# Layer 2 of six chunks as seven half-block products, q's sums from a ones column, and a new written order

## The chip, the core and the metric

The kernel runs on one core of a Trainium2 chip. TensorE (PE) multiplies matrices from SBUF into PSUM; VectorE (DVE), ScalarE (ACT) and GpSimd (POOL) do elementwise work; SyncE (SP) and also ACT and POOL issue DMAs. PEld is TensorE's loading of the stationary operand, which has rows of its own in the profile. The metric is device time of one execution in microseconds (us), median of three runs. Before the change it is 292.93 us (292.82 to 293.19).

## The reference

For each of 8 batches and 8 heads (576 rows, 64 columns), an attention without a softmax over scores:

```python
q_s = softmax(q, axis=-1)            # over the 64 columns of a row
k_s = softmax(k, axis=2)             # over the 576 rows
kv  = einsum('bhsd,bhse->bhde', k_s, v)
a   = einsum('bhsd,bhde->bhse', q_s, kv)
```

The heads side by side make x (8 x 576 x 512). Then comes a feed-forward block:

```python
xn  = (x - mean(x)) / sqrt(var(x) + 1e-6) * g_ln
out = x + relu(xn @ w_ch1) @ w_ch2   # 512 -> 2048 -> 512
```

Inputs and output are float32; the kernel multiplies in bfloat16 and accumulates in float32.

## The kernel before, in words

A batch m is handled as a "side" (attention and normalization, class Side) and a chunk (the feed-forward). A side takes 512 of the 576 rows as four tiles j = 0..3 of 128; the 64 rows left over of batches m-1 and m form a fifth tile (j = 4) of the odd m. The eight chunks 0 to 7 have 512 rows each, and chunk 8 holds the left-over rows of all batches.

A side's steps, by their names in the written order: `kl`, `ql`, `vl` (loads; `kll`, `qll`, `vll` for left-over rows); `kmax`, `kmaxl`, `kar` (maximum of k, across partitions on POOL); `ksub`, `kexp`; `vc` (v to bfloat16, on POOL from batch 2 on); `qmax`, `qsub`, `qexp`; `qTd` (q transposed by a DMA on SP's queue, from batch 2 on); `pkv` (the products k'v, with a ones column in v for k's sums); `kvb` (scaled into `kv_ab`); `zq` (the row sums of exp(q) and their reciprocals: a DVE reduction, L353, and L354; for batches 0 and 1 two-column products `zpe` on PE and a reciprocal, L366); `po` (q times kv, L419 and L428, into one PSUM bank); `x` (L442, which divides by q's sums and writes x in bfloat16 and its row sum); `xn` (x minus its mean; DVE or ACT); `sq` (L466, ACT, sum of squares); `xT`/`xTd` (the transpose, by DMA from batch 2 on, L502); `rstd` (L506, L507).

A chunk's steps: `l1.c.m` (L538: four matmuls of 128 x 512 into one PSUM bank, for each of 16 groups m of 128 hidden columns; chunks 0 and 1 in smaller parts, L552); `relu` (L544, ACT, into `hT`); `l2.c.t` (L592: for each of four row tiles 16 matmuls of 512 columns, in four steps); `put` (L602, DVE: PSUM times rstd, minus x, which is held negated); `store` (one 256 KB DMA per tile). The normalization's rstd is thus applied at the end, in `put`, and no step before layer 2's end waits for it. Chunk 8 ends with three pieces of its last tile (L570, L578).

Nothing is scheduled by a tool while the kernel is built. The string PROGRAM lists every step, and the engines receive their instructions in that order, each engine's queue in order. `warm` steps are matmuls whose result nobody reads. `gate` steps are tiny DMAs on SP's queue that read a few elements of a tile, so that SP's queue waits until the tile is there. PSUM's eight banks are two rings of four (`mm_ps` for the feed-forward, `sm_ps` for the sides); v's float32 tile (`vin`) has two buffers, the output tile (`otp`) four.

Of the kernel before, what the change touches and what calls it, by code (L numbers as in the profile page):

```python
# [20 lines left out]
def kernel(  # L21
# [13 lines left out]
    P = 128  # L35
# [9 lines left out]
    INV = 1.0 / DM  # L45
    HALVED = ()
# [7 lines left out]
    ZPE = 2  # L54
# [39 lines left out]
    kv_ab = const.tile([P, 4, KO1, P], BF16)  # L94
# [33 lines left out]
    class Side:  # L128
# [199 lines left out]
        def qT_heads(self, c0, c1):  # L328
            ptr = self.ptr[c0] = sm_ps.tile([P, J, c1 - c0, P], BF16, tag="sm", name="ptr")
# [26 lines left out]
        def zpe(self, a, n):  # L356
            zp = self.zps[a] = sm_ps.tile([P, n, H], FP32, tag="sm", name="zp")
# [10 lines left out]
        def qT(self, a, n):  # L368
            ptr = self.ptr[a] = sm_ps.tile([P, n, KO1, P], BF16, tag="sm", name="ptr")
# [14 lines left out]
        def pkv(self, c0, c1):  # L384
            if c0 in (a for a, b in self.kvparts):
                self.pk = sm_ps.tile([P, KO1, KVW], FP32, tag="sm", name="pk")
# [14 lines left out]
        def kvb(self, a, b):  # L401
# [3 lines left out]
            for e in range(2):  # L405
                r = slice(64 * e, 64 * e + 64)
                nc.vector.tensor_mul(
                    kv_ab[r, self.m % 4, a:b, 64 * e:64 * e + 64], pk[r, a:b, :D],
# [3 lines left out]
        def po(self, j, ps=None):  # L412
            ps = ps or sm_ps
            pot = self.pot[j] = ps.tile(
                [P, H, D], FP32, tag="sm" if ps is sm_ps else "mm", name="pot"
            )
            if j < J:
                for c in range(KO1):
# [3 lines left out]
                        kv_ab[:, self.m % 4, c, :], start=True, stop=True,  # L422
                    )
            else:
                for b in (self.m - 1, self.m):
                    r = rows(b)
                    for c in range(KO1):
                        nc.tensor.matmul(  # L428
                            pot[r, 2 * c:2 * c + 2, :],
                            qTl[:, c, r],  # L430
                            kv_ab[:, b % 4, c, :], start=True, stop=True,
                        )

        def x(self, j):

            m = self.m
            if j < J:
# [3 lines left out]
            xs = xs_ab[:, m, j:j + 1]  # L441
            nc.vector.scalar_tensor_tensor(  # L442
                xt.rearrange("p (h d) -> p h d", h=H), in0=self.pot[j], scalar=-1.0,
                in1=rq[:, :, None].to_broadcast([P, H, D]),
# [4 lines left out]
        def xn(self, eng, j):  # L449

            xt, xs = self.xs[j]
            if eng is nc.scalar:
                eng.activation(  # L453
                    xn_ab[:, j], xt, AF.Identity, bias=xs, scale=-float(DM)
                )
            else:
                eng.tensor_scalar(
                    xn_ab[:, j], in0=xt, scalar1=-float(DM), scalar2=xs,
                    op0=ALU.mult, op1=ALU.add,
# [10 lines left out]
        def xT(self, a, n, c0=0, c1=KO1):  # L470
            pxt = self.pxt[a, c0] = sm_ps.tile([P, n, c1 - c0, P], BF16, tag="sm", name="pxt")
# [32 lines left out]
    def rstd_of(ci):  # L504
        ln = sm2.tile([P, J], FP32, tag="ln")
        nc.scalar.activation(ln, ssq[:, ci], AF.Ln, bias=eps_ln, scale=INV)  # L506
        nc.scalar.activation(rstd[:, ci], ln, AF.Exp, scale=-0.5)  # L507
# [26 lines left out]
    def l1(ci, m):  # L534
        src = xnT_ab[:, ci % 2] if ci < B else xnTl
        ph = phs[ci, m] = mm_ps.tile([P, SM], FP32, tag="mm", name="ph")
# [9 lines left out]
    def l1_part(ci, c, t, n):  # L546

        ph = phs[ci, c, t] = mm_ps.tile([P, 4 // n, n * P], FP32, tag="mm", name="ph")
# [14 lines left out]
    pcs = {}  # L563

    def l2_last(i):

        c, n = LAST[i]
        pcs[i, "last"] = mm_ps.tile([P, n], FP32, tag="mm", name="pc")
# [6 lines left out]
    def put_last(i):  # L575
        c, n = LAST[i]
        o = ots[i, "last"] = otp.tile([P, DM], FP32, tag="ot", name="ot")
        nc.vector.scalar_tensor_tensor(  # L578
            o[:, :n], in0=pcs[i, "last"], scalar=rstd[:, B, 3:], in1=xl[:, 3, c:c + n],
            op0=ALU.mult, op1=ALU.subtract,  # L580
        )

    def store_last(i):
        c, n = LAST[i]
        for eng, b in ((nc.sync, B - 2), (nc.scalar, B - 1)):
            eng.dma_start(out[b, SM:, c:c + n], ots[i, "last"][rows(b), :n])

    def l2(ci, ti, kos):
        if kos[0] == 0:
            pcs[ci, ti] = mm_ps.tile([P, DM], FP32, tag="mm", name="pc")  # L590
# [6 lines left out]
    ots = {}  # L597

    def put(ci, ti):
        xt = x_ab[:, ci % 2, ti] if ci < B else xl[:, ti]  # L600
        ots[ci, ti] = otp.tile([P, DM], FP32, tag="ot", name="ot")
        nc.vector.scalar_tensor_tensor(  # L602
            ots[ci, ti], in0=pcs[ci, ti], scalar=rstd[:, ci, ti:ti + 1], in1=xt,
# [3 lines left out]
    def store(eng, ci, ti):  # L607
        if ci in HALVED:
            dst = out[ci, (ti // 2) * 2 * P:(ti // 2 + 1) * 2 * P, :]
            eng.dma_start(dst.rearrange("(p j) c -> p j c", j=2)[:, ti % 2, :], ots[ci, ti])  # L610
        elif ci < B:
            dst = out[ci, :SM, :].rearrange("(p j) c -> p j c", j=J)
            eng.dma_start(dst[:, ti, :], ots[ci, ti])
        else:
            for b in (2 * ti, 2 * ti + 1):
                eng.dma_start(out[b, SM:, :], ots[ci, ti][rows(b)])

    def warm(n, width):

        for i in range(n):  # L620
            nc.tensor.matmul(
                idle[:, :width], ident, kv_ab[:, 3, :width // P], start=True, stop=True
# [23 lines left out]
        relu.0.1.0 l1.0.0.2 sq.0.1 qT.1.0 relu.0.1.2 l1.0.8.0 relu.0.0.2 l1.0.9.0 kmax.1.0
        l1.0.11.0 relu.0.9.0 relu.0.8.0 l1.0.10.0 relu.0.11.0 qTe.1.0@DV l1.0.13.0 relu.0.10.0
# [534 lines left out]
```

## Time and profile before

| | |
|---|---|
| median of three runs | 292.93 us (292.82 to 293.19) |
| span of the profiled execution, which is its own time from first to last instruction | 291.7 us |
| PE | 282.4 us busy |
| DVE | 182.0 us busy |
| ACT | 171.7 us busy |
| POOL | 45.9 us busy |
| granted TensorE clock | 0.999 |
| first matmul of chunk 0's layer 1 | at 21.2 us |
| last matmul of chunk 8 ends | at 287.6 us |

A group's row gives its line, engine and operation, what it writes and reads, the shape and the count, then the busy time and the mean duration of one, and after the bar how long the engine was idle before them and who ended that idle time. A matmul's duration includes the pipeline behind it, so the time from one matmul to the next is read from the chain of work: a piece of 16 matmuls that takes 3.45 us has one every 216 ns. DVE's groups add up to some 193 us where its busy time is 182.0: two instructions in a row overlap by about 36 ns. Times outside the span (some 1.2 us between span and median) are the same program's start and end.

### The profile page before, as it was taken

What the parts mean: (1) busy time and instruction counts of PE and PEld (TensorE: products, weight loads), DVE (VectorE), ACT (ScalarE), POOL (GpSimd) and SP (SyncE); (2) the same over time, 40 slices, a digit from 0 to 9 for tenths busy, and PEclk for the clock granted to TensorE, in tenths of its full rate; (3) what the DMA queues carried; (4) which work ended last, traced back from release to release, by engine and by line L of the source; (5) the groups of instructions that cost most, each with busy time, mean ns of one, the idle gap of its engine ahead of it and who ended that gap; (6) DMA issues with size and microseconds to landing.
All of it is one profiled execution on the core that took longest, in us unless ns stands there. A gap on an engine that the chain in (4) does not pass through costs nothing.

```text
span 291.7 us, 4966 instructions
## 1 busy us (share of the span) xinstructions
PE 282.4 (97%) x1923; PEld 145.8 (50%) x1952; DVE 182.0 (62%) x309; ACT 171.7 (59%) x322; POOL 45.9 (16%) x48
## 2 busy tenths in 40 slices
PE   6999999999999999999999999999999999999994
PEld 2479445756444544554454444544544444444443
DVE  6988696997999978988859759614520410220022
ACT  1578793587868885795485638860787077017400
POOL 1810420080421030115130300300000000000000
PEclk9999999999999999999999999999999999999999
DMA  7999999997989999697899759366202331110015
GB/s 213 332 247 237 237 223 298 353 227 205 218 225 216 310 190 246 151 277 170 231 175 281 215 128 235 53 91 143 76 18 51 77 125 39 67 40 36 2 30 115
DMA packets 78144, 49.62 MB, mean 170 GB/s; under 512 B 44580, under 2 KB 73640, under 8 KB 78120
## 3 DMA queue, kind: packets, MB, share of 16 engines
q1 hardware_dynamic: 61008, 34.75, 49.0%
q10 hardware_dynamic: 12888, 10.36, 12.3%
q0 software_dynamic: 4224, 4.19, 8.5%
q8 instruction: 15, 0.25, 0.4%
q14 instruction: 9, 0.07, 0.1%
HBM read 36.70 MB, written 9.44 MB: 158 GB/s over the span
## 4 chain that ended last, share of the span: by engine, by line
PE 74%; DMA 16%; DVE 2%; SPq 2%; ACT 2%; POOL 1%; issue 1%; POOLq 0%
PE pc L592 37%; PE ph L538 27%; DMA w_sb<-in_moe_w_ch_dram 8%; PE ph L552 5%; DMA qt<-in_q_dram 4%; DMA vt<-in_v_dram 3%; PE pot L419 2%; PE pk L394 1%; DMA vl<-in_v_dram 1%; PE pc L570 1%; POOL v_ab L109 1%; SPq L382 1%; DVE qm L295 1%; ACT hT L544 1%; DVE x_ab L442 1%
## 5 line engine op out<-in xcount | busy, mean ns | idle before, releaser
L592 PE MATMUL pc<-w_sb,hT 128*128 128x512 bf16 x544 | 122.8, 379 | 1.3 <-DMA w_sb<-in_moe_w_ch_dram 0.2
L544 ACT ACTIVATE hT<-ph 128x512 bf16<-128x512 f32 x112 | 63.3, 595 | 60.8 <-PE ph L538 59.9
L538 PE MATMUL ph<-xnT_ab,w_sb 128*128 128x512 bf16 x374 | 86.0, 379 | 0.4
L592 PEld LDWEIGHTS <-hT 128*128 128x128 bf16 x560 | 54.1, 98 | 64.3 <-DMA w_sb<-in_moe_w_ch_dram 0.7
L538 PEld LDWEIGHTS <-w_sb 128*128 128x128 bf16 x448 | 42.9, 98 | 49.0 <-issue 0.2
L602 DVE SCALAR_TENSOR_TENSOR ot<-pc,rstd,x_ab 128x512 f32<-128x512 f32 x32 | 23.2, 746 | 44.4 <-PE pc L592 32.9
L199 POOL PARTITION_ALL_REDUCE km<-kmx x10 | 17.0, 1697 | 88.7 <-DVE kmx L194 63.0
L552 PE MATMUL ph<-xnT_ab,w_sb 128*128 128x128 bf16 (+2 forms) x254 | 29.1, 272 | 0.1
L442 DVE SCALAR_TENSOR_TENSOR x_ab<-pot,rq 128x512 bf16<-128x512 f32 x32 | 20.9, 686 | 12.6 <-PE pot L419 12.4
L466 ACT ACTIVATE xsq<-x_ab,xs_ab 128x512 bf16<-128x512 bf16 x32 | 22.9, 715 | 6.3 <-issue 4.7
L552 PEld LDWEIGHTS <-w_sb 128*128 128x128 bf16 x256 | 19.7, 98 | 8.3 <-DMA w_sb<-in_moe_w_ch_dram 0.2
L109 POOL CAST v_ab<-vt 128x1024 bf16<-128x1024 f32 x14 | 18.7, 1356 | 23.3 <-DMA vt<-in_v_dram 23.2
L241 ACT ACTIVATE ek_ab<-kt 128x1024 bf16<-128x1024 f32 x14 | 14.5, 1051 | 10.8 <-DVE kt L217 10.7
L217 DVE TENSOR_TENSOR kt<-kt,km 128x1024 f32<-128x1024 f32 x14 | 17.7, 1275 | 3.7 <-POOL km L199 3.7
L559 ACT ACTIVATE hT<-ph 128x512 bf16<-128x512 f32 x32 | 17.5, 597 | 3.7 <-PE ph L552 3.7
L295 DVE TENSOR_REDUCE qm<-qt 128x16 f32<-128x1024 f32 x14 | 16.8, 1208 | 3.0 <-DMA qt<-in_q_dram 3.0
L453 ACT ACTIVATE xn_ab<-x_ab,xs_ab 128x512 bf16<-128x512 bf16 x23 | 15.7, 713 | 4.9 <-DVE x_ab L442 4.9
L300 DVE TENSOR_TENSOR qt<-qt,qm 128x1024 f32<-128x1024 f32 x14 | 17.8, 1274 | 0.2
L602 DVE SCALAR_TENSOR_TENSOR ot<-pc,rstd,xl 128x512 f32<-128x512 f32 x3 | 2.2, 748 | 22.0 <-PE pc L592 22.0
L305 ACT ACTIVATE eq_sb<-qt 128x1024 bf16<-128x1024 f32 x14 | 14.7, 1050 | 1.2 <-DMA xnT_ab<-xn_ab 1.0
L353 DVE TENSOR_REDUCE sumq<-eq_sb 128x16 f32<-128x1024 bf16 x12 | 14.4, 1201 | 0.0
L538 PE MATMUL ph<-xnTl,w_sb 128*128 128x512 bf16 x63 | 13.9, 379 | 0.1
(87 smaller groups left out, 203.7 us busy)
## 6 DMA issues: line engine op xcount, KB each, us to landing
qt<-in_q_dram SPq DMA_DIRECT2D x6, 1024.0 KB, 9.3
kt<-in_k_dram SPq DMA_DIRECT2D x5, 1024.0 KB, 7.2
vt<-in_v_dram SPq DMA_DIRECT2D x5, 1024.0 KB, 9.2
out_dram<-ot SPq DMA_DIRECT2D x20, 256.0 KB, 3.4
w_sb<-in_moe_w_ch_dram POOLq DMA_DIRECT2D x8, 512.0 KB, 15.9
out_dram<-ot ACTq DMA_DIRECT2D x12, 256.0 KB, 3.3
kt<-in_k_dram ACTq DMA_DIRECT2D x2, 1024.0 KB, 11.9
vt<-in_v_dram ACTq DMA_DIRECT2D x2, 1024.0 KB, 9.9
```

The lines of the kernel that those rows point to most:

```text
L109: eng.copy(dst, src) if eng is nc.scalar else eng.tensor_copy(dst, src)
L217: eng.tensor_tensor(a, a, b, op=ALU.subtract)
L295: nc.vector.tensor_reduce(t, self._q(a, n), axis=AX.X, op=ALU.max)
L300: eng.tensor_tensor(x, x, t[:, :, :, None].to_broadcast([P, n, H, D]), op=ALU.subtract)
L442: nc.vector.scalar_tensor_tensor(xt.rearrange("p (h d) -> p h d", h=H), in0=self.pot[j], scalar=-1.0, in1=rq[:, :, None].to_broadcast([P, ...
L466: nc.scalar.activation(xsq, xt, AF.Square, bias=xs, scale=-float(DM), accum_out=s)
L538: nc.tensor.matmul(ph, w1_sb[:, ko, m * P:(m + 1) * P], src[:, ko, :], start=(ko == 0), stop=(ko == KO1 - 1),)
L544: nc.scalar.activation(hT[:, m, :], phs[ci, m], AF.Relu)
L552: nc.tensor.matmul(ph[:, i], w1_sb[:, ko, m * P:(m + 1) * P], xnT_ab[:, ci % 2, ko, t * P:(t + n) * P], start=(ko == 0), stop=(ko == KO1 - 1),
L559: nc.scalar.activation(hT[:, c * (4 // n):(c + 1) * (4 // n), t * P:(t + n) * P], phs[ci, c, t], AF.Relu)
L592: nc.tensor.matmul(pcs[ci, ti], hT[:, ko, ti * P:(ti + 1) * P], w2_sb[:, ko, :], start=(ko == 0), stop=(ko == KO2 - 1),)
L602: nc.vector.scalar_tensor_tensor(ots[ci, ti], in0=pcs[ci, ti], scalar=rstd[:, ci, ti:ti + 1], in1=xt, op0=ALU.mult, op1=ALU.subtract,)
```

## The change

In chunks 2 to 7 (`QUICK`) layer 2 is computed by half blocks. Rows (512), the inner dimension (2048) and columns (512) are each halved. Eight products of 256 x 1024 by 1024 x 256 would give the four output blocks; the change forms seven products (`term` 1 to 7; Strassen's scheme in Winograd's form). Each is 16 matmuls of 256 columns, eight inner blocks for two row tiles. For that,

- four sums or differences of halves of `hT` (`sum.c.n.g`, in two parts g of 128 x 1024 bfloat16 on DVE, eight instructions a chunk) and, once, four of the halves of `w_ch2` (`ws`, 128 x 2048 bfloat16; three on POOL, one on DVE);
- the seven products go to three PSUM banks: products 1, 6, 7 and 4 add up in u, 2 in a, 5 and 3 in b. Between them DVE reads u minus x four times (`less`) and adds a or b three times (`plus`), all 128 x 512; each next product into u waits for the `less` that reads the one before;
- `put` falls away in these chunks, and rstd is multiplied in by `xn` instead. So `xn` waits for `rstd` of the four tiles and for two small instructions (`sc`, on POOL or DVE) in chunks 2 to 7;
- two stores of 512 KB a chunk replace four of 256 KB, and a `less` waits until the last chunk's store has read the output tile, of which there is now one per row tile.

For batches 1 to 7, q's sums come from a ones column in `kv_ab` (65 columns a head instead of 64): `po` writes 130 columns a matmul, over two PSUM banks, and `x` begins with a reciprocal of eight numbers from PSUM. The `zq` reduction and batch 1's `zpe` go.

The rings of PSUM are replaced by bank numbers in the order itself (`%n`). `vin` has one buffer. The whole PROGRAM is written anew: the layer-1 groups come in another order (in chunk 3: 0, 15, 12, 2, 6, ...), loads move between SP's and ACT's queues, and the gates stand early in SP's queue.

```diff
-            if j < J:
-                xt, rq = x_ab[:, self.sl, j], self.rq[:, j]
...
+            if m == 0:
+                rq = self.rq[:, j, :, None]
             else:
-                xt, rq = xl[:, m // 2], self.rql[:, 0]
+                rq = sm2.tile([P, H, 1], FP32, tag="rq2")
+                nc.vector.reciprocal(rq, self.pot[j][:, :, D:D + 1])
...
+            if ci in QUICK:
+                by, xs = (scale_ab[:, n, ci, i:i + 1] for n in range(2))
...
+    def scale_of(eng, ci, i=0, n=J):
+        r = rstd[:, ci, i:i + n]
+        xs = xs_ab[:, ci, :J] if ci < B else xs_ab[:, 2 * i + 1, J:]
+        eng.tensor_scalar(
+            scale_ab[:, 0, ci, i:i + n], in0=r, scalar1=-float(DM), scalar2=None, op0=ALU.mult
+        )
+        eng.tensor_tensor(scale_ab[:, 1, ci, i:i + n], r, xs, op=ALU.mult)
...
+    SUMS = {3: (S3, A[0][0], A[1][0], ALU.subtract), 2: (S2, A[1][1], S3, ALU.subtract),
+            1: (S1, S2, A[0][0], ALU.add), 4: (S4, A[0][1], S2, ALU.subtract)}
+    WSUMS = {1: (T1, W[0][1], W[0][0]), 2: (T2, W[1][1], T1), 3: (T3, W[1][1], W[0][1]),
+             4: (T4, W[1][0], T2)}
+    TERMS = {1: ("u", A[0][0], W[0][0]), 2: ("a", A[0][1], W[1][0]), 3: ("b", S4, W[1][1]),
+             4: ("u", A[1][1], T4), 5: ("b", S1, T1), 6: ("u", S2, T2), 7: ("u", S3, T3)}
...
+    def sums(eng, n, a, b):
+        o, x, y, op = SUMS[n]
+        eng.tensor_tensor(o[:, a:b], x[:, a:b], y[:, a:b], op=op)
...
+        for ko in range(KH):
+            for i in range(2):
+                nc.tensor.matmul(
+                    quick[ci, where][:, i], s[:, ko, i * P:(i + 1) * P], w[:, ko],
+                    start=first and (ko, i) == (0, 0), stop=(ko, i) == (KH - 1, 1),
...
+    def less_x(ci, where, t, c):
+        i = slice(2 * t, 2 * t + 2)
+        x = (x_ab[:, ci % 2, i] if ci < B else xl[:, i])[:, :, c * NH:(c + 1) * NH]
+        nc.vector.tensor_tensor(part(t, c), quick[ci, where], x, op=ALU.subtract)
+
+    def plus(ci, where, t, c):
+        o = part(t, c)
+        nc.vector.tensor_tensor(o, quick[ci, where], o, op=ALU.add)
...
+        l1.6.9%1 relu.6.1 l1.6.10%2 sum.6.3.0 relu.6.9 sum.6.3.1 relu.6.15 term.6.1%0 relu.6.10
+        sum.6.2.1 qexp.7.4 sum.6.2.0 sq.7.0 qTd.7.4 po.7.3%4 less.6.1 sq.7.1 x.7.3 xT.5.4 term.6.6
+        sq.7.2 sum.6.1.0 sq.7.3 sum.6.1.1 term.6.2%7 rstd.7 less.6.2 sc.7@DV xn.7.2@DV xn.7.3@AC
+        sum.6.4.0 term.6.7 xn.7.0@AC xT.7.3 xn.7.1@DV plus.6.1 xT.7.1 term.6.5%3 less.6.3 xT.7.2
+        term.6.4 plus.6.2 xT.7.0 sum.6.4.1 term.6.3 less.6.4 stores.6.1@AC l1.7.1%1 plus.6.3
...
+        term_of(6, S[2], WT[1], a)
+        b = dve(("less", ci, 2), lambda e: less_x(ci, "u", 0, 1), P[6], kept(ci - 1, 0), kept(ci - 1, 1))
+        term_of(7, S[3], WT[2], b)
+        c = dve(("less", ci, 3), lambda e: less_x(ci, "u", 1, 1), P[7], kept(ci - 1, 2), kept(ci - 1, 3))
+        o22 = dve(("plus", ci, 2), lambda e: plus(ci, "b", 1, 1), P[5], c)
+        term_of(4, relus[1], WT[3], c)
+        term_of(3, S[4], T["w2l", 2], T["w2l", 3], o22)
```

More of the change, by code (lines that the diff above doesn't have):

```diff
@@ new lines @@
+        sum.3.4.0 kmaxl.6.0 qTd.5.2 vc.6.2 term.3.3 qmax.6.0 kar.6.0 qTd.5.0 qmax.6.2 l1.4.5%7
+        qTd.5.3 plus.3.3 l1.4.7%4 ksub.6.1 l1.4.2%5 plus.3.1 l1.4.0%6 relu.4.2 kvb.5.0 stores.3.0@SP
+        relu.4.5 l1.4.11%1 vl.6.0@SP relu.4.0 ksub.6.2 l1.4.9%0 xT.1.4 relu.4.11 less.3.4 ql.7.0@AC
+        l1.4.12%5 relu.4.7 ksub.6.0 l1.4.14%2 relu.4.12 kmax.7.0 l1.4.4%7 l1.4.3%6 relu.4.4 qsub.6.0
+        qexp.3.4 po.5.2%3 l1.4.13%1 relu.4.14 qll.7.0@SP relu.4.3 x.5.2 l1.4.15%5 qTd.3.4 relu.4.13
```

482 lines of the change are left out of this document (288 added, 194 removed).

## The prediction, made before the changed kernel ran

> **What bounds the kernel now.** I read the page's busy times first, then PE's share between its first and last feed-forward matmul, then the chain of work, and last the groups and DVE by stretches of time.
>
> The page's first two parts (busy time, and shares in 40 slices):
>
> ```profile
> PE 282.4 (97%) x1923; PEld 145.8 (50%) x1952; DVE 182.0 (62%) x309; ACT 171.7 (59%) x322; POOL 45.9 (16%) x48
> PE   6999999999999999999999999999999999999994
> DVE  6988696997999978988859759614520410220022
> ```
>
> Busy time by stretches, all engines and then DVE alone:
>
> ```profile
> 21.20:287.60 266.40, 264.29 (x1764) 135.66 (x1791) 163.82 (x269) 161.27 (x306) 36.84 (x28) 1.00 0.69 164
> ...
> 54.00:142.00 88.00, 79.82 (x114) 1.00 0.93 223
> 142.00:196.00 54.00, 36.91 (x63) 1.00 0.74 182
> ```
>
> From 21.2 to 287.6 us PE is idle for 2.1 us in all: PE's work is the time. DVE has slack on average (62%), but until 142 us it is 91% busy (79.82 of 88) without holding PE up. So two numbers are needed: what PE loses, and whether DVE can carry more in the first half.
>
> Pieces of the chain (start, length, what):
>
> ```profile
> 14.24 22.72 DMA w_sb<-in_moe_w_ch_dram
> ...
> 41.08 0.18 PE zp L361 x8
> ...
> 48.35 3.45 PE pc L592 x16
> ...
> 53.98 0.87 PE ph L552 x8
> ```
>
> Matmuls of 512 columns come every 0.2156 us, those of 256 columns (chunk 1's parts) every 0.1087 us, each with a weight load of its own.
>
> Groups (busy, mean of one):
>
> ```profile
> L602 DVE SCALAR_TENSOR_TENSOR ot<-pc,rstd,x_ab 128x512 f32<-128x512 f32 x32 | 23.2, 746 | 44.4 <-PE pc L592 32.9 <-issue 11.0 <-ACT rstd L507 0.3
> L353 DVE TENSOR_REDUCE sumq<-eq_sb 128x16 f32<-128x1024 bf16 x12 | 14.4, 1201 | 0.0
> L184 DVE TENSOR_TENSOR kmx<-kt 128x1024 f32<-128x1024 f32 x7 | 8.5, 1219 | 1.0 <-DMA kt<-in_k_dram 1.0
> L187 DVE TENSOR_TENSOR kmx<-kmx 128x512 f32<-128x512 f32 x7 | 4.8, 692 | 0.2
> L109 DVE COPY qT_sb<-ptr 128x1024 bf16<-128x1024 bf16 x3 | 2.1, 690 | 0.5 <-PE ptr L372 0.5
> L404 DVE RECIPROCAL rz<-pk 128x4 f32<-128x4 f32 x7 | 1.2, 171 | 2.9 <-PE pk L394 2.7
> ```
>
> **PE, which sets the end.** Layer 2 of a chunk is 64 x 0.2156 = 13.80 us; seven products are 7 x 16 x 0.1087 = 12.17 us. Six chunks save 6 x 1.63 = 9.8 us. Batch 1's two `zpe` pieces (0.18 each) save 0.4; `po`'s 130 columns instead of 128 cost under 1 ns a matmul, 0.2 us in all. PE's sum falls by 10.0 us. Against the profiled span that is 291.7 to 281.7; the median stands 1.2 us above the span, so without any new wait it would be 282.9.
>
> **DVE, off the path until now.** Gone: reductions 12 x 1.20 + 4 x 0.67, their reciprocals 3.8, batch 1's two (0.5), 24 `put` x 0.75: 39.4 us. New: 32 reciprocals of eight numbers at 0.2 (between 0.171 for 4 and 0.25 for 16): 6.4; 24 `less` at 0.75 (as `put`, same shapes) and 18 `plus` at 0.69 (L187): 30.4; `sc` on DVE three times, some 0.4 each, and some six more `xn` at 0.35: 3.3; one `ws`, 1.2; and 48 `sum`.
>
> No row shows a two-input bfloat16 instruction in SBUF. From above, a float32 one of as many elements takes 1.22 us (L184); from below, a bfloat16 copy 0.69 (L109). I take 0.69, the row with the same type in and out and the same count, and keep 1.22. Then `sum` is 33.1 us, and DVE goes from 182 to 217 us.
>
> [...]
>
> Where it falls matters more. A middle chunk's words on DVE: `kmax`, `kmaxl` 2.6; `ksub` 3.3; `qmax`, `qsub` 5.0; `kvb` 1.0; four `x` with accumulator read and reciprocal at 0.97, 3.9; two `xn` 0.7; half of a left-over tile 1.5; `sum` 5.5; `less` 3.0; `plus` 2.1. That is 28.6, less 36 ns of overlap for each of some 37 instructions: 27.3 us. PE in the same chunk: layer 1 13.8, products 12.2, `pkv` 0.8, `po` 1.0: 27.8 us. Added up word by word from chunk 1's layer 1 to the end of chunk 5's products, DVE has 140.1 us and PE 141.7. DVE, which managed 91% when nobody waited for it, would have to manage 99%. It cannot: it waits for `rstd` before `sc`, for PE before each `less`. At 96%, 140.1 becomes 145.9 and PE loses 4.2 us; at 93% 8.9; at 99% nothing. I take 96%, because an engine that others wait for seldom stands idle, and its longest waits in a chunk's walk (next) come to about 1 us of 28.
>
> **The joints between products.** Chunk 6, walked with row durations, zero where product 1 starts; DVE is lightly loaded here. Product 1 ends at 1.74 (read by DVE from 1.95), `po.7.3` at 1.96. DVE: `sum.6.2.1` waits for `relu.6.15` to 0.6, then to 1.25; `sum.6.2.0` to 1.9; `less.6.1` 1.95 to 2.68. Product 6 starts at 2.73: PE stands 0.8 us. Then `x.7.3` to 3.6, two sums to 4.9, `less.6.2` to 5.6, ahead of product 7 at 6.2. `sq.7.3` and `rstd.7` on ACT to 5.0, `sc.7` to 6.0, `xn` to 7.45. The four transposes follow one another on SP's queue at 1.22 each from 6.8, the last starting at 10.5; by its row it lands some 2.6 later, at 13.1, and product 3 ends at 13.15. So layer 1 of chunk 7 finds its input just in time. Chunks 2 and 3 walked so give 0.8 to 1.1; in the busy chunks this is the same loss as the 4.2 above, not one on top. For chunk 6 I add 0.8, for chunk 7, whose gaps `l1.8` fills, 0.5.
>
> **What is moved.** `ws` on POOL: 128 x 1024 casts take 1.36 us there, so 2048 elements 2.7, or 5.4 with two inputs; two stand ahead of `kar.2.0`, but start when w_ch2 is in (about 46 us), and `kar.2.0` began at 58.5: no cost either way. SP: `ql.2.0` and the left-over loads (1.4 MB) go ahead of the last weights, behind `vl.1.0`, which shares the saturated engines until 41 us; the chain's 22.7 us of weight DMA says what a delay is worth: zero if they stay behind `vl.1.0` in its queue, 5.8 us at the 245 GB/s of that stretch if they do not. I take zero, as the queue's order is kept. The gates hold SP until about 46 us; the first thing behind them that PE needs, `qTd.2.0`, is written at about 54. `vl` waits for the one `vin` buffer: 9.2 us to land within a chunk's 27: hidden. Stores issued by ACT wait for `plus` and would hold the relus behind them: below 0.5 us a chunk, inside the 96%. The relus of the next chunk's lower half wait for product 7, after which two more products run: hidden.
>
> **Sum.** 292.9 - 10.0 + 4.2 + 1.3 = 288.4 us.
>
> **Rivals.** *Sums at full length* (slower). If `sum` costs 1.22, the 40 before chunk 6 add 21.2 us to a DVE that has nothing left: (140.1 + 21.2)/0.96 is 168, 26 above PE's 141.7, and chunk 6's walk loses 2.7: some 312 us. It decides at 0.8 us a sum, where the 4.5 us gain is gone. Against it: the 0.69 copy. Chance 0.08.
>
> *Late transposes* (slower). rstd now stands ahead of `xn`, and `xT` is the last thing before layer 1. The x transposes of before:
>
> ```profile
> DMA to landing us min/median/max: 2.4/2.7/4.8
> ```
>
> If they land at 4.8, PE waits 2.1 more at each of five joints: 299; it decides at 0.9 each. For it: DMA is 74 to 93% busy there, and the q transposes' longest took 7.9. Against: the median. Chance 0.09.
>
> *Weight loads bound the products*, so that the change doesn't deliver: 112 loads replace 64. Were a load (98 ns) not hidden, a product's matmul would take 0.207 us and six chunks cost 56 us more: 350. Against it, transposes of 128 columns with their loads come at 56 ns. Chance 0.01. [...]
>
> *The order absorbs it*: DVE keeps 99%, and only the 1.3 of chunks 6 and 7 stay: 284.2. Against: no stretch of before shows such a share. Chance 0.10.
>
> **Numbers.** My forecast has 0.72; its own range is 285.6 (97% for DVE, nothing lost in chunks 6 and 7) to 293.1 (93%, and the 1.3). The range 284 to 296 takes in the absorbing order and the mild half of late transposes and leaves out some 0.17: the sums, the loads, the other half of the transposes, and a little of both tails. This kernel's runs spread 0.1%, so 0.2% is about what can be told from no change. Faster: 0.68 of my case and 0.10, 0.78; same 0.04; slower 0.18.
>
> **What would show it.** Right: layer-2 matmuls of 256 columns at 0.109 us; `sum` near 0.69 with `less` and `plus` at 0.7 to 0.75; DVE busy some 217 us, over 93% from 54 to 195; PE idle inside its stretch up from 2 to 7 or 8 us, ended by `less` and `sum`. Wrong: `sum` above 0.8; layer 1 of chunks 3 to 7 waiting for transposes; the first layer-2 matmul later than 37 us.

## The result, and the profile after

| | before | after |
|---|---|---|
| median of four runs | 293.04 us (292.82 to 293.19) | 334.97 us (332.14 to 338.77) |
| ratio | | 1.139, 95% interval 1.134 to 1.145 |
| span of the profiled execution | 291.7 us | 337.0 us |

The change makes the kernel 42 us slower, where 4.5 us faster was forecast. The profiled execution of after is the longest of its four runs (338.77 us, 3.8 above the median), so the difference between the two spans, 45.3 us, is some 3 us more than the one between the medians; what is read from that profile is set beside other kernels below where they share its parts.

The page of after, the totals and two rows of the forty slices:

```profile
PE 287.2 (85%) x2203; PEld 178.1 (53%) x2224; DVE 228.1 (68%) x389; ACT 167.7 (50%) x315; POOL 60.7 (18%) x57
PE   0879999399893859985996899599999999999995
PEclk9999999899997878997799799799999999999999
```

PE no longer runs without a gap: of the slices from 17 to 219 us eleven are under 90% busy, where before none was, and in some of them, or just behind them, the slice's granted clock is down to 0.7 or 0.8. So PE's busy time *rose* by 4.8 us, although the change takes work from it.

Where the time went, by three stretches: first matmul of chunk 0's layer 1, first matmul of its layer 2, first matmul of chunk 2's layer 1, first matmul of chunk 8's layer 2. Columns: stretch, length, busy time of PE, PEld, DVE, ACT and POOL, granted clock, DMA share, GB/s. Before:

```profile
21.20:37.00 15.80, 15.52 (x184) 11.29 (x183) 12.07 (x17) 12.64 (x27) 3.17 (x3) 1.00 1.18 237
37.00:83.80 46.80, 46.42 (x361) 26.59 (x369) 41.79 (x74) 32.49 (x59) 14.07 (x9) 1.00 1.04 250
83.80:273.50 189.70, 188.30 (x1125) 89.73 (x1144) 106.97 (x175) 115.19 (x221) 19.59 (x16) 1.00 0.59 145
```

After:

```profile
29.30:45.10 15.80, 15.26 (x179) 11.28 (x178) 12.53 (x17) 12.42 (x27) 4.21 (x4) 1.00 1.17 236
45.10:106.80 61.70, 48.48 (x355) 27.15 (x359) 53.54 (x80) 34.34 (x65) 25.89 (x12) 0.96 0.71 166
106.80:319.10 212.30, 192.12 (x1419) 122.00 (x1434) 138.47 (x246) 108.97 (x207) 21.37 (x22) 0.94 0.53 127
```

Layer 1 starts 8.1 us late; the way from there to chunk 2 is 14.9 us longer, the way from chunk 2 to chunk 8 another 22.6; the end is 0.3 shorter. These are the 45.3 us between the spans. In the third stretch PE is idle for 20.2 us instead of 1.4, and at a mean clock of 0.94 it needs 192.1 us for work that by the prediction's sum takes some 179 at a clock of 1.00 (188.3 less the form's 9.8).

What ended PE's longest waits in after (total, times, longest):

```profile
PE ps L568 <- DMA xnT_ab<-xn_ab: 11.9, 4, 5.7
PE ps L700 <- POOL ident masks.py:199: 9.9, 1, 9.9
PE ps L496 <- DVE x_ab L463: 5.5, 1, 5.5
PE ps L671 <- DVE ot_sb L683: 4.5, 2, 3.9
PE ps L447 <- ACT hT L574: 3.9, 1, 3.9
PE ps L447 <- DMA qT_sb<-eq_sb: 3.5, 1, 3.5
```

The second is PE's first instruction of all, which waits for `ident`, and POOL makes `ident` with its first instructions. Only the fourth is a joint of the seven products (`less`, L683), and its longest wait stands behind POOL as well. The chain that ended last (`--critical --window 200:330`; start, length, what) has there:

```profile
207.72 3.43 POOLq L1338
211.15 0.19 POOL scale_ab L537
...
213.51 0.61 DVE ot_sb L683
214.16 3.12 PE ps L671 x16
```

`sc.5` on POOL comes late, `xn` on DVE comes after it, and `less` stands in DVE's queue behind `xn`. POOL's timeline (start, length, what, and in brackets how long it stood idle before):

```profile
9.31 0.20 POOL masks.py:197 MEMSET ident<- 128x128 bf16 x1 [8.88 <-issue]
...
54.85 9.04 POOL L661 TENSOR_TENSOR t_sb<-w_sb 128x2048 bf16<-128x2048 bf16 x2 [9.78 <-DMA w_sb<-in_moe_w_ch_dram]
...
105.52 1.80 POOL L216 PARTITION_ALL_REDUCE km<-kmx  x1 [5.93 <-issue]
```

POOL waits 8.88 us at the start and 5.93 us ahead of an all-reduce for nothing that the profile shows; before, the first of these is 0.46 us and the other does not exist. Ahead of two of the three `sc` it waits in the same way, 7.1 and 9.8 us:

```profile
POOL scale_ab L534 <- issue: 16.9, 2, 9.8
```

These waits stand where POOL goes from its all-reduce (`kar`) to `tensor_tensor` and `tensor_scalar` (`ws`, `sc`) or back; what POOL does in them is not shown. In e2 and e3 below such waits are 5.7 to 11.0 us long. And while `ws` runs on POOL, from 54.85 to 63.9, some instructions of DVE take three to twelve times as long:

```profile
54.54 1.22 DVE L312 TENSOR_REDUCE qm<-qt 128x16 f32<-128x1024 f32 x1
...
55.91 0.69 DVE L463 SCALAR_TENSOR_TENSOR x_ab<-ps,rq 128x512 bf16<-128x512 f32 x1
...
56.52 3.47 DVE L317 TENSOR_TENSOR qt<-qt,qm 128x1024 f32<-128x1024 f32 x1
59.91 4.13 DVE L480 TENSOR_SCALAR xn_ab<-x_ab,xs_ab 128x512 bf16<-128x512 bf16 x1
```

`qsub` (L317) takes 3.47 us instead of 1.2 and `xn` (L480) 4.13 instead of 0.35; a reduction (L312, 1.22 us) and `x` (L463, 0.69), which reads PSUM, keep their length. Beside the third `ws` on POOL, from 93.36 to 97.74 us, a step of `kmax` (L204) takes 4.43 us instead of 0.69. What the two engines do to one another there is not shown; in e1 below, with no `ws` on POOL, the longest `xn` of the same kind takes 0.353 us.

### The profile page after: what moved, and what is told of

The parts are those of the page before. It is cut to its first block, busy times and chain, and to the rows that moved or that the text cites. A ratio compares the mean times of both kernels' runs of the same rounds, so it can differ in the third digit from the quotient of the medians.

```text
span 337.0 us, 5623 instructions
## 1 busy us (share of the span) xinstructions
PE 287.2 (85%) x2203; PEld 178.1 (53%) x2224; DVE 228.1 (68%) x389; ACT 167.7 (50%) x315; POOL 60.7 (18%) x57
## 4 chain that ended last, share of the span: by engine, by line
PE 48%; DVE 22%; issue 10%; DMA 10%; ACT 3%; POOL 3%; POOLq 1%; SPq 1%; ACTq 0%; DVEq 0%
PE ps L568 25%; PE ps L671 14%; DMA qT_sb<-eq_sb 4%; PE ps L622 4%; DVE kt L234 3%; DMA xnT_ab<-xn_ab 3%; DMA kl<-in_k_dram 3%; POOL km L216 2%; DVE kmx L204 2%; DVE xn_ab L480 2%; DVE qt L317 2%; PE ps L447 2%; DVE kmx L201 1%; DVE w_sb L549 1%; DVE kl L234 1%
## 5 line engine op out<-in xcount | busy, mean ns | idle before, releaser
L568 PE MATMUL ps<-xnT_ab,w_sb 128*128 128x512 bf16 x372 | 95.1, 408 | 13.7 <-DMA xnT_ab<-xn_ab 11.9
L574 ACT ACTIVATE hT<-ps 128x512 bf16<-128x512 f32 x112 | 60.5, 609 | 79.8 <-PE ps L568 64.8
L568 PEld LDWEIGHTS <-w_sb 128*128 128x128 bf16 x448 | 45.1, 103 | 67.4 <-issue 25.1
L671 PEld LDWEIGHTS <-hT 128*128 128x128 bf16 x384 | 37.8, 99 | 10.3 <-issue 4.1
L622 PE MATMUL ps<-w_sb,hT 128*128 128x512 bf16 x171 | 40.0, 385 | 0.5 <-issue 0.4
L671 PEld LDWEIGHTS <-s_sb 128*128 128x128 bf16 x288 | 28.2, 98 | 4.1 <-issue 0.7
L582 PE MATMUL ps<-xnT_ab,w_sb 128*128 128x128 bf16 (+2 forms) x254 | 29.1, 272 | 0.3 <-ACT hT L589 0.2
L671 PE MATMUL ps<-t_sb,hT 128*128 128x256 bf16 x192 | 24.1, 281 | 4.1 <-DVE ot_sb L683 3.9
L322 ACT ACTIVATE eq_sb<-qt 128x1024 bf16<-128x1024 f32 x14 | 14.6, 1052 | 21.1 <-DVE qt L317 18.6
L671 PE MATMUL ps<-t_sb,s_sb 128*128 128x256 bf16 x192 | 22.3, 272 | 0.5 <-DVE ot_sb L683 0.5
L463 DVE SCALAR_TENSOR_TENSOR x_ab<-ps,rq 128x512 bf16<-128x512 f32 x32 | 22.0, 691 | 1.1
L671 PE MATMUL ps<-w_sb,hT 128*128 128x256 bf16 x192 | 22.4, 273 | 0.0
L683 DVE TENSOR_TENSOR ot_sb<-ps,x_ab 128x512 f32<-128x512 f32 x24 | 16.5, 688 | 8.7 <-PE ps L671 8.6
L317 DVE TENSOR_TENSOR qt<-qt,qm 128x1024 f32<-128x1024 f32 x14 | 19.5, 1392 | 0.2
```

Source lines behind the costliest of these rows:

```text
L317: eng.tensor_tensor(x, x, t[:, :, :, None].to_broadcast([P, n, H, D]), op=ALU.subtract)
L463: nc.vector.scalar_tensor_tensor(xt.rearrange("p (h d) -> p h d", h=H), in0=self.pot[j][:, :, :D], scalar=-1.0, in1=rq.to_broadcast([P, H, ...
L568: nc.tensor.matmul(ph, w1_sb[:, ko, m * P:(m + 1) * P], src[:, ko, :], start=(ko == 0), stop=(ko == KO1 - 1),)
L574: nc.scalar.activation(hT[:, m, :], phs[ci, m], AF.Relu)
L582: nc.tensor.matmul(ph[:, i], w1_sb[:, ko, m * P:(m + 1) * P], xnT_ab[:, ci % 2, ko, t * P:(t + n) * P], start=(ko == 0), stop=(ko == KO1 - 1),
L622: nc.tensor.matmul(pcs[ci, ti], hT[:, ko, ti * P:(ti + 1) * P], w2_sb[:, ko, :], start=(ko == 0), stop=(ko == KO2 - 1),)
```

## The experiments

Three theories. **A**: the waits where POOL goes from its all-reduce to `ws` and `sc` or back, the long wait at its start among them, and the DVE instructions that take longer beside `ws` cost the time. **B**: the seven-product form itself loses it, by its joints and DVE's load. **C**: the places of loads, gates and DMA issues in the new order lose it. The medians of before, measured again beside each of these runs, lie at 293.0 to 293.2 us. The stages of each kernel, from its profile (us):

| kernel | first layer 1 | first layer 2 | chunk 2 | chunk 8, layer 2 | chunk 2 to 8 | median | ratio to before, 95% |
|---|---|---|---|---|---|---|---|
| before | 21.2 | 37.0 | 83.8 | 273.5 | 189.7 | 293.0 | |
| after | 29.3 | 45.1 | 106.8 | 319.1 | 212.3 | 334.97 | 1.134–1.145 |
| e1 none on POOL | 21.8 | 53.4 | 106.3 | 301.6 | 195.3 | 321.75 | 1.096–1.101 |
| e2 sc off POOL | 21.8 | 53.0 | 113.1 | 314.8 | 201.7 | 332.72 | 1.133–1.140 |
| e3 ws off POOL | 32.0 | 47.1 | 101.1 | 307.2 | 206.1 | 324.97 | 1.106–1.110 |
| e4 before + tail add | 31.0 | 46.3 | 92.9 | 282.2 | 189.3 | 302.16 | 1.029–1.032 |
| h1 before, gates early | 21.7 | 52.2 | 98.8 | 288.1 | 189.3 | 307.75 | 1.048–1.053 |
| h2 before, loads early | 21.6 | 45.9 | 92.6 | 281.9 | 189.3 | 301.46 | 1.027–1.032 |
| f1 gate.0 last | 21.8 | 42.8 | 100.2 | 298.8 | 198.6 | 316.34 | 1.072–1.084 |
| f2 and kll.1 on SP | 21.8 | 37.1 | 108.8 | 304.8 | 196.0 | 324.89 | 1.102–1.113 |
| f3 and all gates last | 21.8 | 37.2 | 99.7 | 294.7 | 195.0 | 322.22 | 1.093–1.105 |
| f4 after, gate.0 last | 31.8 | 46.9 | 111.1 | 319.9 | 208.8 | 339.28 | 1.148–1.162 |
| g1 loads late | 21.9 | 37.2 | 105.1 | 299.4 | 194.3 | 326.35 | 1.109–1.116 |
| g3 start as before | 21.7 | 37.8 | 97.4 | 293.1 | 195.7 | 322.56 | 1.097–1.109 |
| g4 ws late | 21.7 | 37.6 | 97.2 | 297.4 | 200.2 | 324.32 | 1.105–1.108 |
| p1: g1 without the form | 21.8 | 37.2 | 102.0 | 305.6 | 203.6 | 331.72 | 1.123–1.136 |
| p3: g3 without the form | 21.9 | 37.6 | 95.1 | 297.9 | 202.8 | 325.37 | 1.108–1.113 |
| b0 old order, no form | 22.0 | 37.6 | 86.7 | 282.3 | 195.6 | 308.72 | 1.051–1.054 |
| b6 b0 with the form, chunks 2–7 | 22.0 | 37.8 | 88.5 | 327.7 | 239.2 | 355.62 | 1.211–1.216 |
| b5 b0 with the form, chunks 3–7 | 21.8 | 37.6 | 86.3 | 319.8 | 233.5 | 346.32 | 1.173–1.183 |

In f3, g1, g3, g4, p1, p3 and the three b kernels, five gates end the program. They follow the last stores on SP's queue, and from chunk 8's layer 2 to the end these kernels take 24.6 to 25.3 us instead of 17.9. So some 7 us of their medians are this arrangement's and none of the change's; among themselves they can be compared, and against the others by the column "chunk 2 to 8".

### POOL

e1, e2 and e3 change only the engines in words of the written order (e1 all six, e2 the `sc` words, e3 the `ws` words); e4 gives the kernel *before* one tiny `tensor_tensor` as POOL's last work:

```diff
-  ws.1@PO ws.3@PO ws.4@PO    sc.2@PO sc.3@PO sc.5@PO
+  ws.1@DV ws.3@DV ws.4@DV    sc.2@DV sc.3@DV sc.5@DV
```

```diff
+        nc.gpsimd.memset(junk, 0.0)
+        nc.gpsimd.tensor_tensor(junk, junk, junk, op=ALU.add)
```

By theory A the author's estimate, made before the runs, was 288 to 294 us for e1, with the first layer 1 at 21 to 22 us, and 300 to 302 us for e4, with POOL's first instructions 8.4 us later (8.88 less 0.46).

> The changed kernel with all four ws and all sc on DVE, so that POOL runs only what it ran before. [...] Theory B (the seven-product form itself overloads DVE and the joints between products): DVE has some 5 us more to do, and the time stays at 330 us or above.

> The changed kernel with the three sc of POOL moved to DVE; the three ws stay on POOL. [...] Theory A: the start is back (first layer-1 matmul at 21 to 22 us, 8.4 us gained), the waits of xn for sc in chunks 3 and 5 are gone (7 to 10 us each), and only what the ws cost is left: 298 to 312 us. Theory B: 330 us or above, since DVE only gets more to do.

> The changed kernel with the three ws of POOL moved to DVE; the three sc stay on POOL. [...] Theory A: the start stays late (first layer-1 matmul at 29 to 30 us), the DVE instructions that stood still for 3 to 4 us while a ws ran on POOL are back at their own length, and the waits for sc stay: 308 to 324 us. Theory B: 330 us or above.

> The kernel before, with one memset and one addition of 128 x 4 elements as POOL's last instructions, after all its work; nothing reads their result. It prices the start alone. [...] Theory B, or if the late start has another cause: 293 us.

e4 came out as theory A has it, just above the 300 to 302 expected: 9.1 us for an instruction that no one waits for. The time is lost at the start, where layer 1 begins at 31.0 us instead of 21.2; how an instruction at the end of the program comes to delay the start is not shown. Its POOL waits:

```profile
POOL ident masks.py:197 <- issue: 10.5, 1, 10.5
...
POOL junk L1154 <- issue: 6.7, 1, 6.7
```

In e1 the start is back at 21.8 us and the time falls by 13.2 us, neither A's 288 to 294 nor B's 330. e2 landed in B's range (332.7; A had 298 to 312), although its start came back as A has it, and e3 just above A's (325.0; 308 to 324). From chunk 2 to 8 e1 is 17.0 us shorter than after (195.3 against 212.3), and e2 and e3 divide that: with `ws` alone on POOL (e2) the stretch is 6.4 us longer than in e1, with `sc` alone (e3) 10.8. The waits of POOL in e3 show why: two of the three `sc` wait where POOL changes its kind of work, and behind each stand `xn`, the transposes and layer 1.

```profile
POOL scale_ab L534 <- issue: 15.7, 2, 8.9
POOL ident masks.py:197 <- issue: 10.7, 1, 10.7
POOL km L216 <- issue: 5.7, 1, 5.7
```

But up to chunk 2, e1 gained nothing (106.3 against 106.8): the 7.5 us won at the first layer 1 were lost twice over before layer 2 (53.4 us against 45.1). So there was a second cause, which POOL's late start had covered. e3 shows the cover: its POOL starts late, and it reaches chunk 2 5 us *ahead* of e1.

### The start: gates and loads

ACT's timeline in e1:

```profile
30.85 1.08 ACT L589 ACTIVATE hT<-ps 128x512 bf16<-128x512 f32 x2 [6.54 <-DMA kt<-in_k_dram]
...
42.31 1.06 ACT L322 ACTIVATE eq_sb<-qt 128x1024 bf16<-128x1024 f32 x1 [9.38 <-DMA gate<-eq_sb]
```

`gate.0`, 32 bytes, stands in SP's queue behind `vl.1.0` (1 MB) and lands 21.1 us after its issue began. It reads `eq_sb`, so `qexp.1.0`, which overwrites it, waits for it, and with it all of ACT's relus. The 6.54 us belong to the issue of `kll.1` on ACT, which stands just before: it begins at 30.19 us, when `kl.1.0` has landed, and by the profile it is this landing that ends the wait. In h2 below it is the landing of `vll.1`, at 32.63 us, so DMA words that are moved ahead of an issue can change whom it waits for. The parts alone, in the kernel before:

```diff
 h1: -  gate.0 ... gate.4 where chunks 2 to 6 are computed
     +  vl.1.0@SP gate.0    kll.1@AC gate.1    relu.0.8.0 gate.2    l2.0.8 gate.4 l2.0.9 gate.3
 h2: -  ql.2.0@AC kll.2@AC kll.3@SP vll.3@AC qll.3.1@AC at their old places
     +  vl.1.0@SP qll.3.1@SP ql.2.0@SP kll.2@SP kll.3@SP vll.3@SP
```

> The kernel before, with only its five gate words moved to where the changed kernel has them. Gate theory: the tiny DMAs stand behind 1 MB loads, and qexp.1.0 on ACT and w1s on DVE, which overwrite what they read, wait for them with all that is queued behind: 300 to 310. If gates cost only where loads stand behind them: 292.5 to 296.

> The kernel before, with ql.2.0 (1 MB) and the left-over loads qll.3.1, kll.2, kll.3, vll.3 (128 KB each) moved to SP's queue right behind vl.1.0, so ahead of the last half of w_ch2. Load theory: 1.5 MB at the 237 GB/s of that stretch are 6.3 us, and the time 297 to 301. If the transfers hide: 292.5 to 294.

h1: 14.7 us for five DMAs of a few bytes, as theory C has it. ACT's wait, and the stretches of 4 us around it (the columns as above):

```profile
ACT eq_sb L305 <- DMA gate<-eq_sb: 15.1, 1, 15.1
```

```profile
28.00:32.00 4.00, 1.62 (x30) 1.45 (x26) 2.77 (x3) 0.00 (x0) 0.00 (x0) 1.00 1.21 214
32.00:36.00 4.00, 0.00 (x0) 0.00 (x0) 0.02 (x1) 0.00 (x0) 0.00 (x0) 0.59 1.17 245
36.00:40.00 4.00, 0.00 (x0) 0.00 (x0) 0.00 (x0) 0.00 (x0) 0.00 (x0) 0.50 1.10 230
40.00:44.00 4.00, 1.08 (x9) 0.98 (x10) 0.01 (x1) 2.19 (x4) 0.00 (x0) 0.50 0.05 10
44.00:48.00 4.00, 3.78 (x13) 1.55 (x13) 1.95 (x3) 2.53 (x7) 2.40 (x2) 0.70 0.01 2
48.00:52.00 4.00, 4.00 (x28) 1.91 (x26) 3.60 (x3) 3.46 (x7) 1.82 (x3) 1.00 0.83 132
```

All engines stand, from 40 us on the DMA engines too (a share of 0.05), since SP issues nothing between the gate (22.1 us) and 41.8. The granted clock falls to 0.50, and in the window from 48 us, some 5 us after PE resumes at 42.9, it is 1.00 again. h2 is 8.4 us slower, more than the 6.3 worked out from bytes, and by another wait: `kll.1`'s issue on ACT begins at 32.63 us, when `vll.1` has landed, 21.5 us after its own issue.

```profile
33.28 1.08 ACT L559 ACTIVATE hT<-ph 128x512 bf16<-128x512 f32 x2 [9.14 <-DMA vl<-in_v_dram]
```

The same undone in the changed kernel:

```diff
 f1, f4: -  vl.1.0@SP kvb.0.0 warm.6.128 gate.0          (f1 from e1, f4 from after)
         +  ... storeh.2 gate.0
 f2:     f1 and  -  kll.1@AC in chunk 0's layer 1   +  vll.1@SP kll.1@SP
 f3:     f2 and  -  gate.1 ... gate.4               +  at the end
 g1:     e1, gates at the end, vl.1.0@SP kll.1@SP, and ql.2.0@AC kll.2@AC kl.2.0@AC kl.3.0@AC
         vl.2.0@AC in chunk 0's layer 2, the left-over loads on SP from chunk 1 on
 g3:     g1 with kll.1@AC at its old place, qll.1.0@AC qll.1.1@AC behind l2.0.12, vll.2 and vl.2.0 a piece earlier
 g4:     g3 with ws.1 ws.3 ws.2 ws.4 behind l2.1.3, l2.1.8, l2.1.12, l1.2.4
```

> The kernel with ws and sc all on DVE (321.75 us), and in it only the word gate.0 moved from its place behind vl.1.0 to the end of the order. Gate theory: gate.0 reads eq_sb, stands in SP's queue behind a 1 MB load, and qexp.1.0 on ACT waits for its landing (9.4 us) with chunk 0's relus behind it; with the gate away the first layer-2 matmul comes near 44 to 46 us instead of 53.4, and the time is 308 to 315. Product theory (the seven-product form itself costs the time): nothing before layer 2 matters, 318 to 323.

> As the one before, and kll.1 issued by SP right behind vll.1 instead of by ACT in the middle of chunk 0, where ACT stood 6.5 us until an earlier load had landed. Gate and issue theory: first layer-2 matmul at 37 to 41 us, no wait of ACT at a DMA issue above 2 us before it, and a time of 298 to 306. Product theory: 316 to 323.

> As the one before, and all five gates at the end of the order. If the later gates, too, hold SP and what stands behind it (ql.2.0, kl.3.0, the transposes of q), 3 to 8 us less than the kernel with gate.0 alone moved: 292 to 302. If they protect the weight loads from the others, 2 to 10 us more, and chunk 0's layer 2 waits for weights.

> The changed kernel with POOL left as it is (ws and sc on POOL), and only gate.0 moved to the end. If gate and POOL each cost their own: 334.97 less the 7 to 13 us that the gate costs without POOL's work, 320 to 328. If POOL's late start hides the gate: 331 to 336.

> The changed kernel with ws and sc on DVE, the five gates at the end of the order, kll.1 issued by SP behind vl.1.0, and the loads of batches 2 and 3 (ql.2.0, kl.2.0, kl.3.0, vl.2.0, kll, qll, vll) at about the places where the kernel before has them, mostly on ACT during chunk 0's layer 2. Load theory (what was lost at the start is 1.5 to 3.5 MB of loads that went ahead of the last weights, and gates that held DVE and ACT): first layer-2 matmul by 41 us, chunk 1's layer 1 by 60 us, and 298 to 308 us in all. If the form itself costs the time: the start may improve, yet 312 to 320.

> The kernel with ws and sc on DVE, the five gates at the end, the loads of batches 2 and 3 at about the old places, and kll.1 on ACT again where the kernel before has it, so that this 128 KB load does not stand behind the 1 MB of vl.1.0. If the start's loss is all a matter of these DMA places: first layer-2 matmul at 36 to 40 us, chunk 1's layer 1 by 58 us, and 300 to 312 us in all (321.75 less the 16 us that the start lost, and some of it lost again to what comes later). If not: first layer-2 matmul after 42, over 316.

> As the kernel above, with the four ws (5 us on DVE) moved from chunk 0's layer 2 and chunk 1's layer 1 to chunk 1's layer 2 and chunk 2's layer 1. If DVE bounds chunk 1: 2 to 6 us below the kernel above. If PE waits for DMAs there: the same within 1.5 us.

None of f1 to g1 came out as expected: f1 (316.3) lies between its two ranges, and f2, f3, f4 and g1 (324.9, 322.2, 339.3 and 326.4) lie in neither of theirs. f1 gained 5.4 us, f4 lost 4.3: in after itself, with POOL late, ACT waits only 2.3 us for the gate, and removing that brings nothing; why f4 is slower is not shown. f2 and f3 brought the first layer-2 matmul to 37.1 us, as expected, and not the end: the weights' second half then lands late (in f3 at 55.8 us, with `ql.2.0` and the left-over loads issued on SP from 26 to 46 us; before, SP issues nothing from 21 to 54), and in f2 `gate.2`, behind `gate.1`, holds `w1s` on DVE until 58.0 us. g1 put those loads back and failed by one 128 KB load: `kll.1`, behind `vl.1.0`, landed 20.4 us after its issue.

```profile
DVE kmx L211 <- DMA kl<-in_k_dram: 9.6, 1, 9.6
```

With that mended (g3) chunk 2 starts at 97.4 us, 8.9 earlier than in e1, still 13.6 later than before. In g3 three issues on ACT, of `kl.3.0`, `vl.2.0` and `qll.1.1`, take 5.2, 4.7 and 3.2 us between 45 and 58 us, and `xn` of chunk 1 stands behind them. The expected 300 to 312 was missed: 322.6, of which 7 are the gates at the end. g4 is no faster (324.3), so DVE's work on `ws` was not what held chunk 1. Theory C holds in the kernel before, where each part has its price alone (h1, h2), and in the changed one only in part: each mended place uncovered the next. What the start costs beyond the parts shown was not brought to nothing by any of these orders.

### The form alone

p1 and p3 are g1 and g3 with layer 2 of chunks 2 to 7 in 16 pieces again, at the places of the seven products, and without `ws` and `sc`:

```diff
-    QUICK = (2, 3, 4, 5, 6, 7)
+    QUICK = ()
-  term.5.1%3 ... term.5.2%0 ... less.5.1 ... term.5.6 ... stores.5.0@SP
+  l2.5.0%3 l2.5.1 ... l2.5.2 l2.5.3 put.5.0 ... l2.5.4%0 l2.5.5 ... store.5.0@SP store.5.1@SP
```

> The same order as the kernel above, but layer 2 of chunks 2 to 7 as before the change (16 pieces of four matmuls in the places of the seven products, put, four stores, no sum, less, plus, ws, sc). The ones column, the bank numbers and the order stay. As predicted for the form (PE 9.8 us less against 4.2 + 1.3 of waits): 3 to 6 us slower than the kernel above. If the form loses more at its joints and to DVE's load than PE gains: 3 to 15 us faster than it.

> As the kernel with the start as before, but layer 2 of chunks 2 to 7 in 16 pieces as before the change and no sum, less, plus, ws, sc. If the form pays what the prediction said (9.8 less 5.5): 3 to 7 us slower than that kernel. If it pays only where DVE waits for something else anyway: the same or faster.

Without the form p1 is 5.4 us slower than g1, within the 3 to 6 expected, and p3 2.8 slower than g3, just under its 3 to 7 (the intervals of the second pair just touch, so its size is uncertain). From chunk 2 to 8 the form gains 9.3 and 7.1 us; up to chunk 2 it gives back 3.1 and 2.3. `ws` on DVE is one difference there, but g4 moved `ws` without a gain, so the reason is open. PE's share of it, g1 and then p1, over that stretch:

```profile
105.10:299.40 194.30, 185.28 (x1419) 119.03 (x1434) 134.76 (x247) 108.81 (x207) 17.00 (x15) 0.98 0.59 140
```

```profile
102.00:305.60 203.60, 194.47 (x1125) 91.30 (x1146) 93.53 (x173) 107.73 (x207) 16.89 (x16) 0.97 0.56 133
```

PE has 9.2 us less to do, and DVE 41 more; from chunk 2 to 8 the stretch is shorter by 9.3 and 7.1 where PE's work fell by 9.2 and 9.0, so the joints and the fuller DVE take no more than 2 us back there. Theory B falls for this order.

The last three put the changed kernel's code (ones column, bank numbers, one v buffer) under the order of the kernel before, b0 without the form, b6 and b5 with it. In these, one row tile of batch 0 is overwritten in its bank before `x` reads it, so that this tile of the output is not the reference's; kind and number of the instructions are unchanged.

```diff
 b0: before's PROGRAM; zq.1 to zq.7, zpe.1 gone; po.m.* 2 pieces apart, x, xn, xT
     with them; pkv.2, pkv.6, kvb, vl.6.0, vll.6 moved; gates at the end; %0-3 for l1, l2; %4-7 for the rest
 b6: -  l2.4.0 ... relu.4.15 ... l2.4.2 ... l2.4.5 ...
     +  term.4.1 relu.4.15 relu.4.14 sum.4.2.1 sum.4.1.1 less.4.1 ... term.4.2 ... term.4.6 less.4.2 ...
     -  xn.4.1@AC ... xT.4.1 ... sq.4.1 ... rstd.4
     +  x.4.0 sq.4.0 ... x.4.2 sq.4.2 rstd.4 sc.4@DV xn.4.0@AC xT.4.0 xn.4.1@DV xT.4.1 ...
```

> The changed kernel's code (ones column, bank numbers, one v buffer) under the order of the kernel before, layer 2 as before in all chunks; the four po of a side stand a little further apart, and the gates at the end. Order theory (the time is lost by where the loads, gates and POOL's work stand, not by the parts): 289 to 297. If the ones column over two banks or the one v buffer cost by themselves: 298 or more.

> As the kernel above, with the seven products in chunks 2 to 7 (their sums, less, plus, rstd and sc ahead of xn; ws and sc on DVE, ws spread over chunk 1 and 2). Order theory with the prediction's price of the form: 4 to 8 us below the kernel above, less some 3 us that chunk 2's late transposes cost, so 284 to 296. If the form loses at its joints: 0 to 15 us above the kernel above.

> As the kernel above, with the seven products in chunks 3 to 7 alone, where DVE has more room. Order theory: 3 to 7 us below the kernel with no products, 284 to 293. If the form loses at its joints everywhere: above it.

b0 (308.7, expected at 298 or more) keeps the start (chunk 2 at 86.7 us) and loses 5.9 us from chunk 2 to 8, without any of the products. PE waits there 3.1 us for relus on ACT ahead of layer 1 and 1.0 ahead of layer 2, against 0.2 in all before. Whether the ones column over two banks, the one v buffer, the bank numbers, the wider `po` or the moved steps bring that was not separated. b6 and b5 are far off what was expected, and show a price that no term of the prediction had. PE's waits in b6:

```profile
PE ps L671 <- ACT hT L574: 15.2, 7, 5.1
PE ps L568 <- ACT hT L574: 12.1, 11, 4.3
PE ps L671 <- DVE ot_sb L683: 10.1, 8, 3.5
```

`sq` and `rstd` now have to be done ahead of `xn`, so they stand in ACT's queue ahead of relus, wait there for `x` on DVE (29.1 us in 13 places in b6), and the relus, the sums and the products wait behind them. Under this one order, which was not tuned further, the form loses 43.6 us in the stretch where it gains 7 to 9 under the rewritten one. So whether the form pays depends on the order around it. That the rewriting, which costs time up to chunk 2, is what lets it pay behind chunk 2 is likely, but these kernels differ from g1 and g3 in the start as well.

## Why the prediction was wrong, step by step

**PE: right.** Products of 16 matmuls come at 1.75 us in the chain (0.109 a matmul), and PE's work in the six chunks fell by 9.2 (g1, p1) and 9.0 us (g3, p3), where 9.8 was worked out. The rival "weight loads bound the products" fell.

**DVE: right in its terms.** `sum` takes 0.67 to 0.69 us, the bound that was taken, `less` and `plus` 0.69:

```profile
L657 DVE TENSOR_TENSOR s_sb<-hT x12: 681/692/693, 129.6 to 296.4; 128x1024 bf16<-128x1024 bf16 x12
...
L683 DVE TENSOR_TENSOR ot_sb<-ps,x_ab x24: 676/692/692, 135.1 to 306.3; 128x512 f32<-128x512 f32 x24
```

217 us busy were predicted. e1 has 220.7, and three more `ws` at 1.2 us each make the difference; after has 228.1, with three instructions of 3.5 to 4.4 us beside `ws` on POOL that take 0.35 to 1.2 elsewhere. The form's net gain was put at 4.3 us and measured at 5.4 and 2.8, but that is in part luck: of the 5.5 us set against it for a full DVE and for joints no more than 1.9 show from chunk 2 to 8, and 2.3 to 3.1 go before chunk 2, where nothing was set. Whether DVE can be kept 96% busy was not tested, as other waits left it gaps (87% in e1 from 54 to 195 us).

**"What is moved": the step that failed.** Its three zeros, for `ws` on POOL, for the loads and for the gates, were wrong, and `sc` on POOL has no term in the sum.
- `ws` on POOL, "no cost either way". The `ws` were priced by their own length, and rightly so (4.4 to 4.5 us each, between 2.7 and 5.4). What was missing: the waits where POOL changes its kind of work (9 to 11 us at the start, 6 to 11 at a later change), and DVE's instructions beside `ws` (3.5 to 4.4 us instead of 0.35 to 1.2). For `sc` on POOL no cost was named at all; without `ws` it costs 10.8 us of the third stretch (e3 against e1).
- "The gates hold SP until about 46 us; the first thing behind them that PE needs, `qTd.2.0`, is written at about 54." That looks only at what stands behind the gates in SP's queue, and in after the last gate is issued at 61.5 us. What the gates read is what others write next: ACT (`qexp.1.0`, 15.1 us in h1) and DVE (`w1s`, 13.8 us in f2) wait for them. The early gates cost 14.7 us in the kernel before; in after, where POOL is late, ACT waits 2.3 us for them.
- "I take zero, as the queue's order is kept", for loads ahead of the last weights. They cost 8.4 us in the kernel before, and by a wait that was not thought of, that ahead of a DMA issue on ACT (9.1 us in h2), an engine whose own work stands behind it.

**The rival "late transposes" happened too.** Layer 1 of later chunks waits 11.9 us in four joints for `xnT_ab`, near the 10.5 that the rival was priced at, but for the most part not for the reason given. The waits ahead of chunks 2 and 3, 7.2 us of it, stand behind `ws` and `sc` on POOL, which `xn` waits for. The 4.0 us ahead of chunk 4, where `sc` is on DVE, are the rival's own reason: the transpose took 6.8 us to land. With none of the words on POOL (e1) 3.6 us are left. The signs that were named did show it: first layer-2 matmul at 45.1 instead of 37, and layer 1 waiting for transposes.

**A cost on top that no step had: the clock.** In after, each of PE's six waits of 3.5 us and more that come after layer 1 began is followed by slices at a clock of 0.7 or 0.8 (in windows of 4 us the lowest behind each is 0.50 to 0.74), so such a gap is paid for again. The product behind the 3.9 us gap takes 3.12 us instead of 1.75. Over the third stretch the clock of 0.94 is worth an estimated 13 us, the 192.1 of busy time less the 179 expected.

Of the 45.3 us, then: 8.1 POOL's start (e4: 9.1 alone); 14.9 up to chunk 2, of which `ws` on POOL is worth 8.4 (from the first layer 1 to chunk 2 after takes 77.5 us and e3, with `ws` on DVE, 69.1; without `sc` on POOL it is 6.8, e2 against e1) and the rest, gates and loads among it, was not divided, since the causes cover one another; 17.0 of the third stretch POOL (after against e1; `ws` alone 6.4, `sc` alone 10.8); and there a remaining 5.6, which is the form's gain of 7 to 9 against 13 to 14 that the rest of the rewriting loses (p1 and p3 against before). What causes this last loss stays open. b0 loses 5.9 under the old order, which shares the code with these kernels but not their order; and late q and x transposes are among what PE waits for in g3:

```profile
PE ps L447 <- DMA qT_sb<-eq_sb: 5.6, 2, 3.9
PE ps L568 <- DMA xnT_ab<-xn_ab: 3.9, 3, 2.8
```

No kernel here beats the one before, so whether the form can stays open.

## What to carry to other kernels

Price a moved instruction not by its length alone but by the waits ahead of it on its engine, by what runs beside it and by what stands ahead of it in its queue: a second kind of work on POOL cost 6 to 11 us at a change here, `xn` took 4.13 us instead of 0.35 beside it, and a DMA of 32 bytes behind 1 MB landed 19.6 us after its issue. For every DMA that changes place, ask which instruction overwrites what it reads and on which compute engine the issue stands: that engine waits with all its queue. And where PE is the bound, count a gap of several microseconds more than once: in after the clock was down, to 0.50 to 0.74 in the lowest window of 4 us, behind each of six gaps of 3.5 to 5.7 us.

## What the runs showed of the hardware

- With a `tensor_tensor` as POOL's last work (e4) the execution is 9.1 us longer, with a wait of 10.5 us ahead of POOL's first instruction after the constants; with `sc` alone on POOL (e3) that wait is 10.7 us, and where no `tensor_tensor` or `tensor_scalar` stands behind the last all-reduce it is 0.5 us (e1, e2), and layer 1 starts at 21.8 us.
- Beside POOL's `tensor_tensor` (after), DVE's `xn` (bfloat16, SBUF to SBUF) takes 4.13 us instead of 0.35 and `qsub` 3.47 instead of 1.2; `x`, which reads PSUM, and a reduction keep their time (0.69 and 1.22 us).
- A DMA of 32 bytes landed 19.6 us after its issue (h1), one of 128 KB after 20.4 and 21.5 us (g1, h2), where 1 MB was ahead of it or beside it.
- In h1 PE stands from 29.6 to 42.9 us. Its granted clock, in windows of 4 us, is 0.59 from 32 us, 0.50 from 36 to 44, 0.70 from 44 and 1.00 from 48.
